# Attention in smaller portions, layers in groups of two units

## The chip, the cores and the metric

The kernel runs on one core of one Trainium2 chip. A core has TensorE (matmuls), VectorE, ScalarE and GpSimd (elementwise work), SyncE (here it issues DMAs), and 16 DMA engines. The metric is the device time of one execution in microseconds (us); less is better.

## The reference

There are three stages. The first is a linear attention with a complex decay: for each of 4 x 8 heads, over 768 steps t,

```python
S_re = ar * S_re - ai * S_im + outer(k[t], v[t])
S_im = ar * S_im + ai * S_re_old
y[t] = q[t] @ S_re
```

where ar and ai are a_re and a_im scaled to a magnitude of at most 0.999, and a head has 48 dimensions. The result is laid out as x, 3072 tokens by 384. The second and third stages are two layers, each with weights of 384 x 2048 and 2048 x 384: `x = softplus(x @ w_in) @ w_out`, then `elu(x @ w_in2) @ w_out2`. All is computed to float32 accuracy, and the weights are given in 64-bit floats.

## The kernel before, in words

Each matmul of the layers is done as three (`Net.PASS`): both operands are split into a high and a low part (`split`, line 398), and high x high, high x low and low x high are added up.

**Units, items, slots.** The 3072 tokens are cut into 12 units of 256. Attention works through the units in order (`decays`, line 849, with `norm`, `prep` and `qk`: products of decays, mostly on VectorE; `chunks`, line 802: its matmuls). One layer for one unit is an item, 24 in all, in the order that `PHASES` (line 421) gives: a triple (m, a, b) is layer m for units a to b - 1. The 2048 hidden columns of an item are done in 8 slots, so the main loop (line 935) runs over 192 slots and two more. Slot n issues the first matmuls of slot n (`s1`, 18 of them), the elementwise work of slot n - 1 (`elem`: ScalarE, then VectorE at line 563 or 566, ScalarE, GpSimd at line 571) and the second matmuls of slot n - 2 (`a_s2`, 18, or `b_s2`, 12). At an item's end `a_out` copies the result and stores it to x2d in DRAM from ScalarE's queue (line 588), or `b_out` stores the final output from SP's. `x_load` (line 921) loads an item's input during the item before, at its third slot, and it is split at its sixth.

**Pace.** `adv(ns)` (line 896) hands out attention: it raises a counter of what is due, and runs attention's generators until the time that `Paced` has added up for attention's VectorE instructions has reached it. `Paced` counts (elements + 70) / 0.96 ns for each (line 27). Each slot calls `adv` twice with `STEP`: twice 2000 ns up to slot 43, twice 1600 from slot 44 (`LATE`) on. Ahead of slot 0 it is called with 6000 (`W0`) until unit 0 is through, with one granule of weights decoded after each call, up to 12. The order in which the program issues instructions is their priority; each engine's own order is made from it by a scheduler when the kernel is built.

**Weights.** A layer's weights are 32 granules of 128 x 384. `w_load` loads one as raw 64-bit floats into one of three raw tiles, wr0 to wr2, `decode` (lines 437 to 444, ScalarE and VectorE) makes a float32 of it, and `w_end` splits it (ScalarE, and GpSimd at line 400). `w_step` does this for the next granule. Four granules make a weight tile w of 1.5 MB, one for each slot of an item; there are eight buffers, so only one layer's weights are held. The first layer's granules are decoded ahead of the slots that need them (line 941). The second layer's are decoded from slot 10 on, at most `R` a slot (line 972), each tile as its buffer comes free. During the first group of each layer `w_store` writes each tile to DRAM (wd, line 500). Whenever the next group of items has the other layer, `w_again` (line 505) reloads the eight tiles during the last item of the group, one a slot, into the buffer just used, six slots ahead of its first use. The first two groups need none, so 48 tiles are reloaded. While no raw granule is in work, attention's decay norm borrows the raw tiles (`more`, line 154; `Net.free`, `Net.spare`).

Of the kernel before, what the change touches and what calls it, by code (L numbers as in the profile page):

```python
# [397 lines left out]
def split(nc, hi, lo, x, eng=None):  # L398
    nc.scalar.activation(out=hi, in_=x, func=AF.Copy)  # L399
    (eng or nc.vector).tensor_tensor(out=lo, in0=x, in1=hi.bitcast(F32), op=ALU.subtract)  # L400
# [7 lines left out]
CH0 = 7  # L408
DLY = 2
W0 = 6000  # L410
STEP = (2000, 1600)
LATE = 44
G0 = 12
GA = 4
R = 3
KT = 7
QT = 0
NS = 2
XU = 2
LD, SP = 2, 5  # L420
PHASES = ((0, 0, 2), (1, 0, 2), (0, 2, 5), (1, 2, 5), (0, 5, 9), (1, 5, 9), (0, 9, 12), (1, 9, 12))


def decode(nc, f, S, raw, odd=None):
# [323 lines left out]
def all_fine(nc, pp, sp, f):  # L748


    for a, b, lim, op in ((0, 12, 2000.0, ALU.is_le), (12, 28, 1e-16, ALU.is_ge), (28, 92, 0.3, ALU.is_le)):
        nc.vector.tensor_scalar(out=f[:, a:b], in0=f[:, a:b], scalar1=lim, scalar2=1.0, op0=op, op1=ALU.mult)
    g, o = f[:, 94:95], f[:, 95:96]
    nc.vector.tensor_reduce(out=g, in_=f[:, 0:92], axis=mybir.AxisListType.X, op=ALU.min)
    nc.vector.memset(o, 1.0)
    nc.tensor.matmul(out=pp[0:1, 0:1], lhsT=g, rhs=o, start=True, stop=True)
    n = sp.tile([1, 1], I32, name="n_fine")
    nc.vector.tensor_copy(out=n, in_=pp[0:1, 0:1])
    return n


def body(tc, q, k, v, a_re, a_im, w_in1, w_out1, w_in2, w_out2, out):
    nc = tc.nc
    keep = tc.tile_pool(name="keep", bufs=1)
    with keep as keep:
        fine = quick(tc, keep, q, k, v, a_re, a_im, w_in1, w_out1, w_in2, w_out2, out)
        n = nc.values_load(fine[0:1, 0:1], min_val=0, max_val=128)
        with tc.If(n < 128):
            general(tc, q, k, v, a_re, a_im, (w_in1, w_out1, w_in2, w_out2), out)


def quick(tc, keep, q, k, v, a_re, a_im, w_in1, w_out1, w_in2, w_out2, out):
    nc = tc.nc
    with ExitStack() as ctx:
# [4 lines left out]
        def bank(n):  # L779
            i = cnt[n] = cnt.get(n, -1) + 1  # L780
            t = nb[n][i % len(nb[n])]
            return psp.tile([128, 512], F32, name=t, tag=t)
# [3 lines left out]
        net = Net(tc, ctx, flags[:, 28:92], bank, ((w_in1, w_out1), (w_in2, w_out2)))  # L786
# [6 lines left out]
        def xparts():  # L793
            return [xp.tile([128, 3, 256], F32R, name=n, tag=n) for n in ("xh", "xl")]
# [101 lines left out]
        def adv(ns):  # L896

            nonlocal due
            due += ns
            while A.vec.ns < due:  # L900
                if next(st, END) is END:
                    due = A.vec.ns
                    return False
            return True
# [11 lines left out]

        items = [(m, u) for m, a, b in PHASES for u in range(a, b)]
        ends = {sum(b - a for _, a, b in PHASES[:i + 1]) - 1: i for i in range(len(PHASES))}
        starts = {0: 0, **{e + 1: i + 1 for e, i in ends.items()}}

        def x_load(m, u):
            t = net.tp.tile([128, 768], F32, name="xr", tag="x2e").rearrange("p (c t) -> p c t", c=3)
            if m:
                src = net.x2d[:, :, u * 256:(u + 1) * 256]
            else:
                while u not in done:
                    adv(1000)
                src = A.st.pop(("xd", u)).rearrange("(c p) t -> p c t", p=128)
            nc.sync.dma_start(out=t, in_=src)
            return t  # L930

        H, G = {}, {}
        acc, xr, fine, more = None, None, None, True
        N = 8 * len(items)
        for n in range(N + 2):
            i, p = n // 8, n % 8
            if n < N:
                m, u = items[i]
                while (m, u) not in X:
                    adv(1000)  # L940
                while net.g < min(32, 4 * n + GA):
                    net.w_step()
                if net.g == 32:
                    net.w_end()
                H[n] = net.s1(m, p, X[m, u])
            el = None
            if 0 <= n - 1 < N:
                el = net.elem(items[(n - 1) // 8][0], H.pop(n - 1))
                next(el)
            more = adv(STEP[n >= LATE])  # L950
            if n >= 2:
                i2, p2 = (n - 2) // 8, (n - 2) % 8
                m2, u2 = items[i2]
                if p2 == 0:
                    acc = [bank("acc0"), bank("acc1")]
                (net.b_s2 if m2 else net.a_s2)(p2, G.pop(n - 2), acc)
                if p2 == 7:
                    if m2:
                        net.b_out(u2, acc, out)
                    else:  # L960
                        net.a_out(u2, acc)
                if starts.get(i2, 9) < 2:
                    net.w_store(8 * m2 + p2)
                j = ends.get(i2, 0) + 1
                if i2 in ends and 2 <= j < len(PHASES):
                    net.w_again(8 * PHASES[j][0] + p2)
                if 8 <= n - 2 and net.g < 64:
                    if net.g == 32 and not net.raw:
                        net.w_load(32)
                        net.w_load(33)  # L970
                    room = 64 if i2 > 1 else 32 + 4 * p2 + 4
                    for _ in range(min(R, room - net.g)):
                        net.w_step()
                if net.g == 64:
                    net.w_end()
            if el:
                next(el)
            more = adv(STEP[n >= LATE])
            if el:
                G[n - 1] = next(el)  # L980
            if n < N and i + 1 < len(items) and items[i + 1] not in X:
                if p == LD and items[i + 1] >= (0, XU):
                    xr = x_load(*items[i + 1])
                if p == SP and xr is not None:
                    X[items[i + 1]] = x = xparts()
                    split(nc, *x, xr)
                    xr = None
            if fine is None and not more and net.g == 64 and net.f is None:
                fine = all_fine(nc, bank("h"), keep, flags)
# [29 lines left out]
```

## Time and profile before

| | us |
|---|---|
| median of 3 runs (lowest to highest) | 1260.63 (1256.4 to 1266.76) |
| the profiled execution, its own time | 1262.47 |
| its span, from the first to the last instruction | 1260.4 |
| TensorE matmuls busy | 1043.7 (83%) |
| VectorE busy | 766.7 (61%) |
| ScalarE busy | 679.9 (54%) |
| GpSimd busy | 358.2 (28%) |
| DMA moved | 216.89 MB, 172 GB/s |
| mean granted clock of TensorE | 0.934 |

The profile is of one execution. PE is TensorE's matmuls and PEld its weight loads, DVE is VectorE, ACT is ScalarE, POOL is GpSimd, SP is SyncE. A line of a stretch gives its start and end, its length, then for PE, PEld, DVE, ACT and POOL the busy time with the number of instructions, the clock granted to TensorE (1.00 is its upper level of 2.4 GHz, 0.50 the lower of 1.2), the busy share of the DMA engines and GB/s. The ends of the stretches are starts of every eighth of the elementwise instructions that lead a slot's work on ScalarE, so a stretch is eight slots of elementwise work or a multiple. A line of the timeline gives start, duration, engine, line, operation, and in brackets the idle time before it and what ended it.

### The profile page before, as it was taken

The page shows a single profiled execution, that of the slowest core. Times are in us where ns is not written, and L with a number is a line of the kernel's source. Part 1 is how long each engine was busy: PE and PEld are TensorE (multiplying, and loading weights), DVE is VectorE, ACT ScalarE, POOL GpSimd, SP SyncE. Part 2 cuts the span into 40 slices and gives each one's busy share as a digit, 9 for nine tenths or more (in the row PEclk, how much of TensorE's full clock was granted, in tenths as well). Part 3 has the DMA queues.
Part 4 walks back from the last instruction along what each step waited for, and adds up shares of the span by engine and source line. Part 5 has one row for each costly group of instructions (what it writes and reads, how often), then busy time and mean ns, then how long its engine had stood idle before and what let it go on. Part 6 is the DMA issues. An engine that isn't in the chain of part 4 may idle for free.

```text
span 1260.4 us, 20406 instructions
## 1 busy us (share of the span) xinstructions
PE 1043.7 (83%) x7914; PEld 1004.9 (80%) x7914; DVE 766.7 (61%) x1329; ACT 679.9 (54%) x1199; POOL 358.2 (28%) x275
## 2 busy tenths in 40 slices
PE   0007698936777899898799799999999999999997
PEld 0006698825667898798798699899999999999997
DVE  4887998879878799898789789411212222112211
ACT  4545657525567466654464445456644445665443
POOL 2433432203344221222232122223232322322322
PEclk9997799867787999899899799999999999999999
DMA  6677755356986963459855898600740047029000
GB/s 157 206 211 247 232 157 150 83 166 193 298 264 211 348 221 90 139 171 323 271 151 139 208 297 240 194 21 19 290 161 26 26 178 273 26 90 349 26 14 16
DMA packets 115722, 216.89 MB, mean 172 GB/s; under 512 B 50849, under 2 KB 86945, under 8 KB 107425
## 3 DMA queue, kind: packets, MB, share of 16 engines
q1 hardware_dynamic: 102496, 206.85, 51.7%
q10 hardware_dynamic: 13120, 8.65, 2.4%
q8 instruction: 64, 1.05, 0.3%
q14 instruction: 42, 0.34, 0.1%
HBM read 154.14 MB, written 61.34 MB: 171 GB/s over the span
## 4 chain that ended last, share of the span: by engine, by line
PE 48%; DVE 17%; DMA 11%; issue 5%; ACT 4%; POOL 1%; SPq 0%; ACTq 0%; DVEq 0%; POOLq 0%
PE b L536 43%; DVE tmp L28 5%; DMA w<-wd 4%; DVE big L28 3%; PE b L329 2%; DMA wr<-in_moe_w_in_dram 2%; DVE wr L28 2%; DVE W L28 1%; DVE X L28 1%; DMA wr<-in_moe_w_out_dram 1%; DMA kT<-dk 1%; DVE f L443 1%; PE b L353 1%; PE b L390 1%; DMA ai<-in_a_im_dram 1%
## 5 line engine op out<-in xcount | busy, mean ns | idle before, releaser
L536 PE MATMUL b<-xh,w 128*128 128x256 f32 x2304 | 451.2, 293 | 32.3 <-ACT w L399 11.6
L571 POOL TENSOR_TENSOR gl<-t,gh 128x512 fp32r<-128x512 f32 x192 | 267.8, 1395 | 706.6 <-ACT gh L569 690.9
L536 PEld LDWEIGHTS b<-xh,w 128*128 128x128 f32 x2304 | 379.5, 199 | 39.0 <-ACT w L399 13.0
L536 PE MATMUL b<-xl,w 128*128 128x256 f32 x1152 | 334.3, 291 | 0.0
L536 PEld LDWEIGHTS b<-xl,w 128*128 128x128 f32 x1152 | 228.9, 199 | 0.9 <-issue 0.9
L536 PE MATMUL b<-w,gh 128*128 128x384 f32 x768 | 203.1, 348 | 27.3 <-ACT gh L569 19.2
L536 PE MATMUL b<-gh,w 128*128 128x256 f32 x1152 | 219.5, 290 | 3.3 <-ACT gh L569 1.7
L569 ACT ACTIVATE gh<-t 128x512 fp32r<-128x512 f32 x192 | 121.2, 631 | 167.1 <-DVE t L563 74.5
L536 PEld LDWEIGHTS b<-gh,w 128*128 128x128 f32 x1152 | 183.4, 197 | 5.0 <-ACT gh L569 2.1
L566 DVE SCALAR_TENSOR_TENSOR t<-t,b 128x512 f32<-128x512 f32 x96 | 65.7, 685 | 186.7 <-ACT t L560 184.7
L536 PE MATMUL b<-gl,w 128*128 128x256 f32 x576 | 164.1, 290 | 2.8 <-POOL gl L571 2.8
L536 PEld LDWEIGHTS b<-w,gh 128*128 128x128 f32 x768 | 139.8, 197 | 29.9 <-ACT gh L569 21.1
L563 DVE SCALAR_TENSOR_TENSOR t<-b,t 128x512 f32<-128x512 f32 x96 | 65.8, 686 | 147.7 <-PE b L536 119.4
L400 POOL TENSOR_TENSOR w<-f,w 128x384 fp32r<-128x384 f32 x64 | 88.6, 1394 | 186.1 <-ACT w L399 186.1
L536 PE MATMUL b<-w,gl 128*128 128x384 f32 x384 | 130.9, 347 | 3.0 <-POOL gl L571 3.0
L536 PEld LDWEIGHTS b<-gl,w 128*128 128x128 f32 x576 | 111.6, 196 | 4.8 <-POOL gl L571 4.1
L291 PE MATMUL b<-eye,big 128*96 128x128 f32 x112 | 20.3, 329 | 110.0 <-DVE big L28 103.7
L559 ACT ACTIVATE t<-b 128x512 f32<-128x512 f32 x96 | 57.0, 595 | 92.1 <-PE b L536 89.3
L291 PEld LDWEIGHTS b<-eye,big 128*96 128x96 f32 x112 | 14.5, 150 | 113.8 <-issue 103.0
L555 ACT ACTIVATE t<-b 128x512 f32<-128x512 f32 x96 | 57.0, 594 | 60.5 <-PE b L536 50.5
L536 PEld LDWEIGHTS b<-w,gl 128*128 128x128 f32 x384 | 74.0, 195 | 5.3 <-POOL gl L571 4.9
L329 PE MATMUL b<-qT,kT 96*128 96x128 f32 x384 | 58.3, 307 | 9.2 <-ACT kT L293 6.1
(112 smaller groups left out, 1457.6 us busy)
## 6 DMA issues: line engine op xcount, KB each, us to landing
w<-wd SPq DMA_DIRECT2D x48, 1536.0 KB
wd<-w SPq DMA_DIRECT2D x16, 1536.0 KB
wr<-in_moe_w_in_dram SPq DMA_DIRECT2D x32, 384.0 KB
wr<-in_moe_w_out_dram SPq DMA_DIRECT2D x32, 384.0 KB
dq<-big SPq DMA_DIRECT2D x12, 768.0 KB
qT<-dq SPq DMA_DIRECT2D x36, 256.0 KB
kd<-big SPq DMA_DIRECT2D x12, 768.0 KB
KN<-kd SPq DMA_DIRECT2D x20, 384.0 KB
```

Source lines behind the costliest of these rows:

```text
L28: return f(*a, **kw)
L291: nc.tensor.transpose(out=ps[0:96, 128 * i:128 * i + 128], in_=W[:, 96 * (4 * g + i):96 * (4 * g + i) + 96], identity=self.eye)
L329: self.nc.tensor.matmul(out=sc[:, h, :], lhsT=KT[:, 4 * g + h, :], rhs=QT[:, 4 * g + h, :], start=(h == 0), stop=(h == 3), skip_group_chec ...
L353: nc.tensor.matmul(out=o, lhsT=V[:, 48 * h:48 * h + 64], rhs=Pt[h // 4][:, h % 4, :], start=(h < 2), stop=(zs is None and h > 5), skip_gro ...
L400: (eng or nc.vector).tensor_tensor(out=lo, in0=x, in1=hi.bitcast(F32), op=ALU.subtract)
L536: self.nc.tensor.matmul(out=out, lhsT=lhsT, rhs=rhs, skip_group_check=True, **kw)
L555: nc.scalar.activation(out=t, in_=h, func=AF.Abs)
L559: nc.scalar.activation(out=t, in_=h, func=AF.Relu, scale=-1.0)
L563: nc.vector.scalar_tensor_tensor(out=t, in0=h, scalar=0.0, in1=t, op0=ALU.max, op1=ALU.add)
L566: nc.vector.scalar_tensor_tensor(out=t, in0=t, scalar=-1.0, in1=h, op0=ALU.add, op1=ALU.max)
L569: nc.scalar.activation(out=gh, in_=t, func=AF.Copy)
L571: nc.gpsimd.tensor_tensor(out=gl, in0=t, in1=gh.bitcast(F32), op=ALU.subtract)
```

## The change

Three settings change, and one condition. `STEP` becomes three steps: twice 2000 ns a slot up to slot 7, twice 900 up to slot 19, twice 1250 after. `PHASES` becomes twelve groups of two items, six of each layer in turn; as every group but the first two is preceded by a reload of eight tiles, 80 tiles are reloaded. `R` falls from 3 to 2. Ahead of the first matmuls of a slot in the second layer, granules are now decoded until that slot's tile is there (36 + 4p of them).

```diff
-STEP = (2000, 1600)
-LATE = 44
+
+STEP = ((8, 2000), (20, 900), (999, 1250))
...
-R = 3
+R = 2
...
-PHASES = ((0, 0, 2), (1, 0, 2), (0, 2, 5), (1, 2, 5), (0, 5, 9), (1, 5, 9), (0, 9, 12), (1, 9, 12))
+PHASES = tuple((m, u, u + 2) for u in range(0, 12, 2) for m in range(2))
...
-                while net.g < min(32, 4 * n + GA):
+                while net.g < min(32, 4 * n + GA) or m and net.g < 36 + 4 * p and net.g < 64:
                     net.w_step()
...
-            more = adv(STEP[n >= LATE])
+            more = adv(next(ns for to, ns in STEP if n < to))
...
-            more = adv(STEP[n >= LATE])
+            more = adv(next(ns for to, ns in STEP if n < to))
```

## Rows read from the trace of the kernel before

**Rows 1.** The page: sums, and busy tenths in 40 slices.
```profile
PE 1043.7 (83%) x7914; PEld 1004.9 (80%) x7914; DVE 766.7 (61%) x1329; ACT 679.9 (54%) x1199; POOL 358.2 (28%) x275
...
PE   0007698936777899898799799999999999999997
...
DVE  4887998879878799898789789411212222112211
```

**Rows 2.** The page, the chain that ended last, by line.
```profile
PE b L536 43%; DVE tmp L28 5%; DMA w<-wd 4%; DVE big L28 3%; PE b L329 2%; DMA wr<-in_moe_w_in_dram 2%; DVE wr L28 2%; DVE W L28 1%; DVE X L28 1%; DMA wr<-in_moe_w_out_dram 1%; DMA kT<-dk 1%; DVE f L443 1%; PE b L353 1%; PE b L390 1%; DMA ai<-in_a_im_dram 1%
```

**Rows 3.** Busy times by stretch: start and end, length, engines (instructions), clock, DMA.
```profile
132.10:197.70 65.60, 54.92 (x451) 51.38 (x450) 63.09 (x107) 40.36 (x76) 22.80 (x16) 0.90 0.56 167
...
397.00:841.80 444.80, 404.41 (x3211) 388.86 (x3212) 362.15 (x618) 238.72 (x393) 107.40 (x73) 0.95 0.68 204
197.70:397.00 199.30, 139.44 (x929) 125.98 (x928) 158.09 (x272) 113.46 (x232) 57.67 (x47) 0.78 0.65 202
...
397.00:480.70 83.70, 75.13 (x537) 72.80 (x538) 74.39 (x131) 53.67 (x90) 22.61 (x16) 0.96 0.72 250
480.70:545.20 64.50, 57.73 (x504) 54.45 (x503) 60.04 (x115) 37.36 (x62) 14.60 (x9) 0.95 0.38 106
545.20:640.40 95.20, 84.61 (x667) 81.63 (x666) 78.33 (x114) 48.81 (x82) 24.68 (x16) 0.95 0.86 267
640.40:688.80 48.40, 46.76 (x371) 44.97 (x370) 47.50 (x82) 24.68 (x41) 10.51 (x7) 1.00 0.47 119
688.80:787.50 98.70, 87.33 (x649) 85.12 (x648) 83.34 (x158) 49.16 (x81) 23.95 (x16) 0.91 0.88 252
787.50:841.80 54.30, 52.85 (x496) 49.89 (x495) 18.55 (x23) 25.04 (x44) 11.06 (x9) 1.00 0.45 123
841.80:876.40 34.60, 34.60 (x291) 34.60 (x290) 6.95 (x9) 21.41 (x36) 10.42 (x9) 1.00 0.07 24
876.40:945.00 68.60, 68.60 (x541) 68.60 (x541) 13.33 (x18) 37.76 (x63) 21.16 (x17) 1.00 0.55 208
945.00:978.80 33.80, 33.80 (x242) 33.80 (x241) 7.46 (x10) 16.11 (x26) 10.35 (x8) 1.00 0.07 24
...
1218.00:1260.40 42.40, 35.75 (x246) 35.43 (x244) 6.61 (x10) 15.87 (x26) 10.33 (x8) 0.96 0.06 21
```

**Rows 4.** Source line 353, attention's output matmuls: durations in ns, first and last start.
```profile
L353 PE MATMUL b<-P,V x384: 270/273/477, 101.0 to 826.7; 128*64 128x128 f32 x192
```

**Rows 5.** Instruction groups of all the span: the first layer's elementwise sum, the decode.
```profile
L563 DVE SCALAR_TENSOR_TENSOR t<-b,t 128x512 f32<-128x512 f32 x96 | 65.8, 686 | 147.7 <-PE b L536 119.4 <-ACT t L557 28.3
...
L443 DVE SCALAR_TENSOR_TENSOR f<-wr,f 128x384 int32<-128x384 int32 x64 | 43.9, 691 | 0.7
L444 DVE SCALAR_TENSOR_TENSOR f<-wr,f 128x384 int32<-128x384 int32 x64 | 39.7, 625 | 0.6
L441 DVE TENSOR_SCALAR f<-wr 128x384 int32<-128x384 int32 x64 | 38.1, 600 | 35.4 <-DMA wr<-in_moe_w_in_dram 14.8 <-POOL w L400 11.1 <-DMA wr<-in_moe_w_out_dram 9.5
```

**Rows 6.** Timeline of ScalarE from 602; below, busy times of two stretches there.
```profile
602.38 0.52 ACTq L588 DMA_DIRECT2D x2d<-x2e  x1
602.95 0.84 ACT L141 ACTIVATE wr<-wr 128x768 f32<-128x768 f32 x1 [11.63 <-DMA w<-wd]
...
591.00:601.40 10.40, 6.30 (x30) 5.81 (x30) 4.38 (x8) 0.32 (x2) 0.00 (x0) 0.84 1.08 256
601.40:608.20 6.80, 3.35 (x11) 3.09 (x12) 2.54 (x4) 4.38 (x8) 1.28 (x1) 0.50 1.02 311
```

**Rows 7.** Timelines of VectorE (decode, two products) and of SP (one load).
```profile
243.78 0.36 DVE L441 TENSOR_SCALAR f<-wr 128x384 int32<-128x384 int32 x1 [2.58 <-DMA wr<-in_moe_w_in_dram]
...
268.60 0.96 DVE L28 TENSOR_TENSOR W<-ar,wr 128x768 f32<-128x768 f32 x1
...
283.66 0.63 DVE L441 TENSOR_SCALAR f<-wr 128x384 int32<-128x384 int32 x2 [8.17 <-DMA wr<-in_moe_w_out_dram]
...
270.45 0.36 SPq L484 DMA_DIRECT2D wr<-in_moe_w_out_dram  x1
```

## The prediction

> **What bounds the kernel now.** I read the slices of the page first, to see where TensorE is not full: its digit is 9 all along only from the 24th slice on, and two slices later the digit of VectorE falls from 9 to 4 and then 1 [rows 1]. So there are two regimes, with attention and without it. Then I read the busy times by stage, cut at the first elementwise instruction of ScalarE of every eighth slot, and last the chain, to learn which waits end late: 43% of the span hangs on the two layers' matmuls and 4% on the reload of weights, w<-wd [rows 2].
>
> Without attention, eight slots (an item) take 34.6 us in the first layer and 33.8 (33.9 over several) in the second, TensorE is busy all of that time at a granted clock of 1.00, and this is so with a reload (68.6 us for two items) as without one [rows 3]. That is the floor. With attention, 397.0 to 841.8, nine items take 444.8 us: VectorE is busy 362 us of them, the DMA engines 68%. Worst are slots 8 to 23, where the second layer's weights are decoded: 199.3 us for 16 slots, with VectorE busy 158 us, TensorE 139 us at a mean clock of 0.78 [rows 3].
>
> What does a matmul of attention cost? The stage from 787.5 has 496 TensorE instructions where a plain one has 288 (36 a slot), and 18.3 us more busy time, so 0.089 us each [rows 3]. The page counts 7914 matmuls [rows 1], of which 12 x 288 + 12 x 240 = 6336 are the layers', so attention has about 1578, some 131 for each of its 12 units.
>
> **How the work is handed out.** The counter of line 27 gives 32.1 us for a unit up to the seventh and 33.8 after, 393.6 in all; 72.9 of it are handed out when slot 0 starts. Before: 44 slots at 4.0 us take 176, the other 144.7 go at 3.2 a slot, which ends at slot 89; the trace's last attention matmul, at 826.7, lies in slots 88 to 95, so the count holds [rows 3, 4]. After: 8 slots at 4.0 (32.0), 12 at 1.8 (21.6), the other 267.1 at 2.5, which ends at slot 127. The real time on VectorE is longer. Of its 766.7 us [rows 1], 192 elementwise instructions of the layers take 0.686 each, 131.7, the decode's three instructions 121.7 (1.9 us a granule) [rows 5], splits and output copies about 33; 480 are left, 1.22 times the counter.
>
> **The change stage by stage.**
>
> Start and slots 0 to 7: the same pace, 132.1 + 65.6 us as now [rows 3].
>
> Slots 8 to 23. Handed out are 32.0 instead of 64.1 us of attention, so VectorE loses 32.1 x 1.22 = 39 us and has 158 - 39 = 119 us. The decode keeps its 32 granules, two a slot, and the new loop adds two more ahead of the matmuls in each of slots 21, 22 and 23, since 32 + 2 x 11 = 54 granules are issued by the end of slot 20 and slot 21 needs 56. The first matmuls of these slots wait for a decode just issued; behind them on TensorE stand the second matmuls of two slots back, and ScalarE and GpSimd wait in turn. Lower bound: VectorE's 119 us. Upper bound: those 119, the 41 us in which it idles now, and 5 for the three late slots, 165. I take 145, near the share that VectorE is busy now (119 / 0.79 = 150), a little less because TensorE needs only about 68.5 + 12 us here.
>
> Slots 24 to 127 (13 items, six of the first layer, seven of the second). TensorE: 6 x 34.6 + 7 x 33.9 = 445 us, and nine of the twelve units, 1183 x 0.089 = 105 us: 550. VectorE: 257 x 1.22 + 13 x 7 = 405 us, so it no longer sets the time. What is lost on top? I take each stage of rows 3 with attention, less its items' floor and its matmuls' 0.089 us. The three pairs of items with a reload lose 83.7 - 68.5 - 0.8 = 14.4 us (from 397.0), 95.2 - 68.5 - 12.4 = 14.3 (from 545.2) and 98.7 - 68.5 - 10.8 = 19.4 (from 688.8); the three single items lose 10.7, 2.8 and 1.2. In the first pair VectorE is busy 89%, a limit that thinner attention lifts. The second pair shows the other kind: ScalarE is idle for 11.63 us, until a reload has landed, and only then, at 602.38, issues the store x2d<-x2e that its copies had made ready [rows 6]. From 591.0 to 608.2 TensorE is idle for 7.6 us, and after the gap the granted clock is 0.50 for 6.8 us [rows 6].
>
> The new order of layers has a reload in every second item, 80 instead of 48, and seven of these windows lie in the attention stretch, where there were three; the last of them, slots 122 to 129, only by half, so I count 6.5. What does a window carry? Two plain items with a reload hold 0.55 of the DMA engines, without one 0.07, so eight tiles cost (0.55 - 0.07) x 68.6 = 33 us, 4.1 each; the single item from 480.7 gives (0.38 - 0.07) x 64.5 = 20 us for 28.7 us of the counter, 23 a unit [rows 3]. A window of eight slots at 5.2 us, 42 us, then has 33 + 8 x 2.5 / 32.8 x 23 + 3 = 50 us of transfers, about as overfull as today's (33 + 18 + 3 in some 47 us). So thinner attention doesn't empty it. A tile issued six slots (31 us) ahead still arrives, since only 8 us pile up; late are small transfers behind the reloads. All of them but ScalarE's stores stand in SP's one queue: qT, kT, KN, x's load and the next raw inputs wait behind a reload that waits for its slot's matmuls. I take 9 us a window, what the second pair's one stall cost with its slow clock (7.6 us idle and part of 3.4): 58 us. Bounds: 20 us in all, if an item loses 1.5 us, between the 1.2 and the 2.8 of the two best single items, and 126 at 19.4 a window. Sum 550 + 58 = 608.
>
> By the Trainium skill ("DMA: Bandwidth & Descriptors", section "Issuing engines are not separate DMA queues"), transfers issued by different engines run on the same 16 DMA engines and interleave. That speaks against more reloads, since another queue gives no way around them; but it would also let ScalarE's small store go between the reload's packets. The trace agrees with the first, while the 11.63 us stand before the issue and so aren't interleaving; by the rule alone the windows would cost little, and the sum would be the first rival's.
>
> Slots 128 to 191: eight plain items, 4 x 34.6 + 4 x 33.9 = 274 us, and 8.5 us of tail (the last item takes 42.4) [rows 3]. Three reloads here hide as now. The store of x2d now comes one slot ahead of the load that reads it in every group, as before in the first alone; between that load and its use lie six slots, 26 us, so I cost it at nothing; without that cover it would be a plain slot, 4.3 us, six times. Unit 3 is the tight one: it is done at slot 33 by the counter and its load is issued at slot 34.
>
> Sum: 132.1 + 65.6 + 145 + 608 + 282.5 = 1233.2 us of span. The profiled execution took 1262.47 us for a span of 1260.4, 2.1 more, and is 1.8 above the median of 1260.63; so about 1234 against the median, 2.1% less.
>
> **The rivals.** *Windows that cost nothing.* If thin attention leaves VectorE and ScalarE so much room that small waits don't reach TensorE, the loss is the lower bound, 20 us: 1195. For it speaks that pairs without attention lose nothing; against it, the 50 us of transfers in 42.
>
> *Reloads as the bound (slower).* Every window costs what the worst costs now, 19.4 us: 676 for slots 24 to 127, 1301 in all. The place is SP's queue and ScalarE's store at the end of a window, where attention's loads and the store stand behind eight tiles. It decides from 13.1 us a window on ((1260.4 - 132.1 - 65.6 - 145 - 282.5 - 550) / 6.5): above that the change is a loss. All three of today's pairs are above it, two of them by little (14.4 and 14.3); against it speaks that VectorE, busy 82 to 89% in them, is part of what they lose, and falls to about 70%.
>
> *The pace doesn't shorten the decode.* VectorE decodes a granule at 243.78 and the next ones at 283.66 [rows 7]: the raw tile of the next granule is lent to attention's decay norm, and the load is issued at 270.45, after the two products that read it (from 268.60). Those products lie at about 128 us of the counter, slot 14 before and slot 21 after. If attention must run that far first anyway, the 86 us up to 283.7 stay, and 31 granules at 2.4 us and the rest make 89 more: 175 us, 1263 in all, no change. Against it: VectorE is free to run that attention early while the decode waits, and TensorE has less to do meanwhile.
>
> **How the numbers follow.** Forecast 0.43, free windows 0.20, decode no shorter 0.17, reloads as the bound 0.20. A measurement of this kernel tells about 1% from no change. The forecast's own range is 1212 to 1256 (slots 8 to 23 between 130 and 160, windows between 7 and 11.5 us), of which a quarter lies above 1248. Of the decode case I put 0.02 to faster and 0.04 to slower, since the rest of its sum has the same spread. So faster by over 1%: 0.32 + 0.20 + 0.02 = 0.54; slower by over 1%: 0.20 + 0.04 = 0.24; the rest, 0.22, within 1%. The range reaches down to the free windows and up to a part of the reload case: 1188 to 1288.
>
> **What would show it.** Right: the stage of slots 8 to 23 at 130 to 160 us with VectorE still its busiest engine; the last attention matmul in slots 127 to 130; VectorE's digits at 6 to 8 up to there; no plain item over 35 us; in the attention stretch a TensorE loss that stands beside DMA shares near 1 and ScalarE's stores. Wrong: a stretch of 13 items under 580 or above 650 us, or a decode stage above 170.

## The result, and the profile after

The change makes the kernel faster: median 1222.99 us (1222.02 to 1228.1, 4 runs) against 1259.8 for the kernel before, a ratio of 0.9709 with a 95% interval of 0.9659 to 0.9759. The profiled execution took 1222.02 us for a span of 1220.3, 40.1 less than before. The forecast was 1234. It was near, but two of its stages were wrong, with opposite signs.

The page of the changed kernel: sums, two rows of slices, and the chain by line.

```profile
PE 1029.5 (84%) x7914; PEld 994.2 (81%) x7914; DVE 769.8 (63%) x1329; ACT 678.1 (56%) x1199; POOL 361.4 (30%) x275
...
PE   0007699937776999999999899999999999999997
...
DVE  4898998888877899595599999881222112221121
...
PE b L536 30%; DMA xr<-xd 1%; PE b L329 1%; DMA V<-in_v_dram 1%; DVE big L28 1%; PE b L353 1%; PE b L390 0%; PE b L356 0%; DVE t L563 0%; DVE W L28 0%; DVE tmp L28 0%; ACT big L233 0%; ACT t L555 0%; ACT t L556 0%; DVE xl L400 0%
```

TensorE's digits are 9 from the 14th slice to the last but one, with one 8 among them; in [rows 1] this is so from the 24th on, with one 7 among them, in the 26th. The dip of slices 9 to 13 stays. The chain can't be set beside [rows 2]: it can be followed back only to 768.5 us, so it tells nothing of the slots before. What the profile has of waits for a reload (w<-wd) in the whole span is below, sum in us, times, longest: two lines of the kernel before, then the only one of the changed kernel, though 80 tiles are reloaded there instead of 48.

```profile
ACT wr L141 <- DMA w<-wd: 11.6, 1, 11.6
PE b L536 <- DMA w<-wd: 2.7, 2, 2.0
```

```profile
ACT gh L569 <- DMA w<-wd: 3.8, 1, 3.8
```

VectorE's digit falls to 1 at 824 us (the 28th slice of 30.5 us), and at 819 before (the 27th of 31.5).

Busy times by stretch of the changed kernel, columns as in [rows 3]: the four stages (slots 0 to 7, 8 to 23, 24 to 127, the rest), then the pairs of items from slot 24 on.

```profile
129.40:194.40 65.00, 52.96 (x443) 49.52 (x442) 62.50 (x107) 39.97 (x75) 22.95 (x16) 0.92 0.57 168
194.40:388.30 193.90, 138.05 (x930) 125.07 (x928) 158.01 (x272) 113.58 (x234) 59.83 (x47) 0.77 0.67 207
388.30:938.60 550.30, 530.68 (x4232) 517.13 (x4233) 393.03 (x656) 307.52 (x506) 151.95 (x105) 0.98 0.76 254
938.60:1220.30 281.70, 275.33 (x2116) 275.01 (x2114) 55.21 (x76) 149.44 (x244) 82.68 (x64) 1.00 0.46 171
...
388.30:467.50 79.20, 73.60 (x517) 71.95 (x518) 71.45 (x120) 48.97 (x82) 25.85 (x17) 0.94 0.75 263
467.50:545.70 78.20, 76.23 (x617) 75.12 (x616) 62.29 (x119) 52.01 (x87) 24.22 (x17) 1.00 0.68 239
545.70:634.10 88.40, 83.53 (x667) 80.49 (x667) 61.06 (x107) 48.96 (x82) 23.59 (x17) 1.00 0.75 240
634.10:733.40 99.30, 94.95 (x782) 92.92 (x781) 94.82 (x153) 56.27 (x92) 25.23 (x17) 0.97 0.87 277
733.40:809.90 76.50, 73.79 (x575) 71.47 (x574) 70.33 (x118) 42.00 (x70) 20.84 (x15) 1.00 0.74 257
809.90:890.40 80.50, 80.37 (x682) 78.95 (x681) 22.98 (x29) 40.43 (x69) 21.94 (x17) 1.00 0.74 249
890.40:972.70 82.30, 82.30 (x681) 80.31 (x680) 16.97 (x25) 39.84 (x66) 20.14 (x16) 1.00 0.61 204
```

The same stage, slots 24 to 127, in the kernel before:

```profile
397.00:978.80 581.80, 541.41 (x4278) 525.86 (x4279) 389.88 (x655) 314.00 (x515) 149.33 (x105) 0.96 0.59 183
```

So the gain lies almost whole in slots 24 to 127, 581.8 to 550.3: TensorE idles 550.3 - 530.7 = 19.6 us of them instead of 581.8 - 541.4 = 40.4, and its busy time is 10.7 lower, at a clock of 0.98 instead of 0.96 and with 46 matmuls less (this stage has one item of the first layer less now). The start took 2.7 us less, the stage of the decode 5.4; the rest is as it was.

Where the time came from shows best at the point where attention has left VectorE. Before, at slot 96 (841.8 us), nothing of attention was left [rows 3]. Now, at slot 104 (809.9 us), VectorE has 14 of attention's 893 instructions left: 31.9 us sooner and eight slots further, which is 34 us of plain slots. Against that stand 324 matmuls of attention still to be done (the groups below), at 0.089 us 29 us, which TensorE takes with almost no idle time (80.37 of 80.50 us, 82.30 of 82.30). 31.9 + 34 - 29 = 37, nearly all of the span's gain of 40. These late matmuls are a tail of attention that hardly needs VectorE. TensorE's attention groups from slot 104 to 127 in the changed kernel:

```profile
L353 PE MATMUL b<-P,V 128*64 128x128 f32 x96 | 10.8, 283 | 0.0
L329 PE MATMUL b<-qT,kT 96*128 96x128 f32 x80 | 10.4, 277 | 0.0
L356 PE MATMUL b<-qT,zs 96*48 96x128 f32 x80 | 8.8, 273 | 0.0
L390 PE MATMUL b<-V,KN 128*96 128x48 f32 x68 | 6.7, 248 | 0.0
```

### The profile page after: what moved, and what is told of

Its sections match the earlier page's. It is cut to its first block, busy times and chain, and to the rows that moved or that the text cites. A ratio compares the mean times of both kernels' runs of the same rounds, so it can differ in the third digit from the quotient of the medians.

```text
span 1220.3 us, 20476 instructions
## 1 busy us (share of the span) xinstructions
PE 1029.5 (84%) x7914; PEld 994.2 (81%) x7914; DVE 769.8 (63%) x1329; ACT 678.1 (56%) x1199; POOL 361.4 (30%) x275
## 2 busy tenths in 40 slices
DMA packets 120329, 267.22 MB, mean 219 GB/s; under 512 B 51360, under 2 KB 87456, under 8 KB 107936
## 5 line engine op out<-in xcount | busy, mean ns | idle before, releaser
L536 PE MATMUL b<-xh,w 128*128 128x256 f32 x2304 | 445.9, 291 | 32.9 <-DVE t L563 10.7
L536 PEld LDWEIGHTS b<-xh,w 128*128 128x128 f32 x2304 | 375.5, 198 | 39.7 <-ACT w L399 12.1
L536 PE MATMUL b<-w,gh 128*128 128x384 f32 x768 | 198.4, 342 | 7.7 <-ACT gh L569 6.5
L566 DVE SCALAR_TENSOR_TENSOR t<-t,b 128x512 f32<-128x512 f32 x96 | 65.6, 684 | 179.0 <-ACT t L560 176.8
L536 PEld LDWEIGHTS b<-w,gh 128*128 128x128 f32 x768 | 136.4, 192 | 9.6 <-ACT gh L569 7.3
L291 PEld LDWEIGHTS b<-eye,big 128*96 128x96 f32 x112 | 15.2, 153 | 109.0 <-issue 102.4
```

Of the source, the lines that this page charges most:

```text
L291: nc.tensor.transpose(out=ps[0:96, 128 * i:128 * i + 128], in_=W[:, 96 * (4 * g + i):96 * (4 * g + i) + 96], identity=self.eye)
L536: self.nc.tensor.matmul(out=out, lhsT=lhsT, rhs=rhs, skip_group_check=True, **kw)
L566: nc.vector.scalar_tensor_tensor(out=t, in0=t, scalar=-1.0, in1=h, op0=ALU.add, op1=ALU.max)
```

## The experiments

Twelve kernels, all timed against the kernel before, whose median was between 1256.87 and 1259.66 in these runs. The table gives what was read of each: the median, the ratio with its interval, the lengths of slots 8 to 23, of slots 24 to 127 and of the rest in the profiled execution, TensorE's idle time in slots 24 to 127 (length less busy time), and the sum of ScalarE's waits of over 1 us just ahead of a store (lines 371 and 588, over the whole span, from the end of ScalarE's instruction before it to the issue).

| kernel | us | ratio (95%) | 8-23 | 24-127 | rest | TensorE idle | store waits |
|---|---|---|---|---|---|---|---|
| before | 1259.8 | 1 | 199.3 | 581.8 | 281.6 | 40.4 | 13.4 |
| after | 1222.99 | 0.9709 (0.9659 to 0.9759) | 193.9 | 550.3 | 281.7 | 19.6 | 4.4 |
| e1 pace alone | 1241.66 | 0.9855 (0.9812 to 0.9899) | 195.3 | 566.0 | 281.3 | 32.7 | 10.2 |
| e2 order alone | 1253.69 | 0.9944 (0.9921 to 0.9966) | 195.2 | 579.1 | 282.0 | 40.4 | 7.9 |
| e3 decode alone | 1273.96 | 1.0109 (1.0077 to 1.0141) | 219.3 | 569.8 | 281.4 | 41.7 | 21.3 |
| e4 nothing lent | 1218.22 | 0.9673 (0.9633 to 0.9713) | 159.9 | 570.5 | 281.7 | 25.3 | 4.5 |
| e5 pace and order | 1222.56 | 0.9723 (0.9684 to 0.9763) | 194.8 | 551.9 | 281.8 | 20.7 | 6.0 |
| e6 late pace 1600 | 1236.96 | 0.9839 (0.9798 to 0.9879) | 194.1 | 567.7 | 282.2 | 35.1 | 15.2 |
| e7 late pace 1000 | 1238.9 | 0.986 (0.9819 to 0.9901) | 191.0 | 541.7 | 306.4 | 30.6 | 25.8 |
| e8 nothing lent, R 3 | 1222.62 | 0.9717 (0.9674 to 0.9759) | 165.7 | 577.3 | 281.9 | 29.4 | 2.9 |
| e9 late pace 1100 | 1239.54 | 0.9847 (0.9821 to 0.9873) | 193.3 | 544.2 | 302.3 | 27.3 | 6.3 |
| e10 groups 2, 2, 4, 4 | 1242.45 | 0.987 (0.9833 to 0.9906) | 194.8 | 566.7 | 282.1 | 30.4 | 16.0 |
| e11 a bump in the pace | 1242.72 | 0.9876 (0.985 to 0.9902) | 194.8 | 565.8 | 282.0 | 33.5 | 16.3 |
| e12 nothing lent, 1100 | 1231.35 | 0.9788 (0.9759 to 0.9818) | 159.8 | 565.5 | 302.5 | 35.7 | 19.0 |

**The parts alone.** In the kernel before, the new `STEP` with its two calls of `adv`:

```diff
-STEP = (2000, 1600)
-LATE = 44
+STEP = ((8, 2000), (20, 900), (999, 1250))
```

> The kernel before with the new pace alone. Theory A (the pace only sets who goes first; VectorE does attention ahead in any case, and the layers' instructions now come first in slots 24 to 127): 1230 to 1248 us, slots 8 to 23 again near 195 us, less TensorE loss after them. In the old groups units 2 to 4 are due at slots 26, 34 and 42 and force some of the old pace there, so not all of the gain of the whole change. Rival B (the order of the layers is what helps, by spreading the dates on which units are due): within 6 us of 1260.

1241.66: the pace alone carries about half of the gain, 15.8 us of it in slots 24 to 127, as Theory A has it; slots 8 to 23 are only 4 shorter. In the kernel before, the new `PHASES` alone:

```diff
-PHASES = ((0, 0, 2), (1, 0, 2), (0, 2, 5), (1, 2, 5), (0, 5, 9), (1, 5, 9), (0, 9, 12), (1, 9, 12))
+PHASES = tuple((m, u, u + 2) for u in range(0, 12, 2) for m in range(2))
```

> The kernel before with six groups of two units of each layer alone, at the old pace. Theory A: attention still goes first up to slot 89, five reloads fall into it, and the time is 1255 to 1285 us. Rival B (the order is what helps): 1220 to 1245 us.

1253.69, just under the one range and far from the other. The 32 tiles more that are reloaded cost nothing that shows, even at the old pace: slots 24 to 127 take 579.1 us instead of 581.8, at a DMA share of 0.75 instead of 0.59, and TensorE idles the same 40.4. In the kernel before, the decode's part alone:

```diff
-R = 3
+R = 2
...
-                while net.g < min(32, 4 * n + GA):
+                while net.g < min(32, 4 * n + GA) or m and net.g < 36 + 4 * p and net.g < 64:
```

> The kernel before with two granules a slot and the new condition alone. Theory A (the decode of slots 8 to 23 is held by a lent raw tile and then by its own chain, not by how many granules a slot may issue): 1256 to 1264 us, slots 8 to 23 at 190 to 203. Rival C (fewer granules a slot let attention and the layers through): those slots under 185 us, 1245 or less.

1273.96, which neither expected: alone this part makes the kernel 1.1% slower. Busy times of e3 in slots 8 to 23 and 24 to 127, then those of attention on VectorE alone (source line 28: its busy time and count, the clock, the DMA share, GB/s) in the first of them:

```profile
195.80:415.10 219.30, 146.10 (x977) 130.81 (x977) 187.58 (x345) 124.53 (x247) 63.31 (x46) 0.77 0.66 203
415.10:984.90 569.80, 528.15 (x4236) 513.49 (x4232) 354.00 (x583) 302.24 (x501) 150.07 (x106) 0.98 0.58 179
```

```profile
195.80:415.10 219.30, 130.64 (x229) 0.77 0.66 203
```

The same reading for the kernel before and then for the changed one:

```profile
197.70:397.00 199.30, 90.10 (x158) 0.78 0.65 202
```

```profile
194.40:388.30 193.90, 90.23 (x158) 0.77 0.67 207
```

A thinner decode lets attention go ahead of it: 229 instead of 158 instructions of attention run on VectorE in slots 8 to 23, 40 us more, and the stage is 20 us longer. The stage after it gets 12 of these back. The two other readings are the most telling of the study: before and after, VectorE ran the same 158 instructions of attention in this stage, though the changed kernel handed out half as much.

**Both together.** The changed kernel with the decode's part undone:

```diff
-R = 2
+R = 3
...
-                while net.g < min(32, 4 * n + GA) or m and net.g < 36 + 4 * p and net.g < 64:
+                while net.g < min(32, 4 * n + GA):
```

> The changed kernel with three granules a slot and without the new condition: pace and order of layers alone. Theory A (with a thin pace VectorE's attention is a filler, so it doesn't matter how many granules a slot may issue): 1218 to 1230 us, slots 8 to 23 at 190 to 198. Rival C (two granules a slot are what the thin pace needs): 1235 us or more.

1222.56, the changed kernel's time, so beside the new pace the decode's part neither costs nor gives. Pace and order are the change; together (35 us, against the 1257.39 timed beside them) they bring more than their parts (18 + 6).

**Why slots 8 to 23 don't shorten.** VectorE decodes a granule of the second layer at 239.35 and the next one at 276.41. The changed kernel's timelines of VectorE and of SP:

```profile
239.35 0.39 DVE L441 TENSOR_SCALAR f<-wr 128x384 int32<-128x384 int32 x1
...
262.82 0.96 DVE L28 TENSOR_TENSOR W<-ar,wr 128x768 f32<-128x768 f32 x1
263.69 0.95 DVE L28 TENSOR_TENSOR W<-ai,wr 128x768 f32<-128x768 f32 x1
...
276.41 0.63 DVE L441 TENSOR_SCALAR f<-wr 128x384 int32<-128x384 int32 x2 [1.87 <-DMA wr<-in_moe_w_out_dram]
```

```profile
264.67 0.35 SPq L484 DMA_DIRECT2D wr<-in_moe_w_out_dram  x1
```

It is the pause of [rows 7], 37.1 us instead of 39.9: the raw tile is lent to attention's decay norm, and its load is issued once the products that read it are through. So in the changed kernel attention was no longer to borrow the raw tiles before the decode is over:

```diff
-        return 32 <= self.g and not self.raw
+        return 64 <= self.g and not self.raw
```

> The changed kernel, but the raw tiles are lent to attention's decay norm only after all 64 granules are decoded, no longer between the two layers' decodes. Theory D (the pause of 37 us in the decode, from 239 to 276, comes from the lent tile): the pause falls under 15 us, slots 8 to 23 take 160 to 178 instead of 194 us, and the time is 1190 to 1210. Rival E (attention must run that far first anyway, or the raw loads are late by themselves): the pause stays and the time is 1218 to 1230.

1218.22: not the total that Theory D expected, but the rival's (at its lower edge), while the stage shortened as Theory D says. Busy times of e4 in slots 8 to 23 and 24 to 127:

```profile
198.20:358.10 159.90, 118.04 (x786) 106.78 (x785) 144.79 (x255) 104.46 (x222) 61.66 (x46) 0.82 0.70 213
358.10:928.60 570.50, 545.25 (x4376) 529.77 (x4377) 403.65 (x666) 313.79 (x517) 154.38 (x106) 0.98 0.77 253
```

The stage falls from 193.9 to 159.9, so lending was worth 34 us of it. The pause under 15 us did not come, though: the one from 239 to 276 is gone, but another stands earlier. VectorE's timeline in e4:

```profile
172.18 0.34 DVE L441 TENSOR_SCALAR f<-wr 128x384 int32<-128x384 int32 x1
...
216.71 0.36 DVE L441 TENSOR_SCALAR f<-wr 128x384 int32<-128x384 int32 x1 [3.15 <-POOL w L400]
```

Two granules are decoded early, the second at 172.18; the third comes at 216.71, after GpSimd's split of the first, and from there on the decode runs, 60 us sooner than in the changed kernel, but with 4.8 us from granule to granule instead of 3.6. But 144 matmuls of attention fewer (930 - 786) run in the shorter stage. They come later, 4376 against 4232: 144 x 0.089 = 13 of the 20 us by which slots 24 to 127 grow, and TensorE's idle time is 6 more. Slots 0 to 7 grow by 4 too. The profiled span is 10 us shorter, the median 5 us, and the intervals overlap: e4 is not clear of the changed kernel. With R = 3 as well:

```diff
-R = 2
+R = 3
...
-        return 32 <= self.g and not self.raw
+        return 64 <= self.g and not self.raw
```

> The changed kernel without lending raw tiles between the two decodes, and with three granules a slot. Theory D (without the lent tile the decode starts when the first weight buffers come free, and then VectorE's share for it sets its speed): three granules a slot put decode ahead of attention, slots 8 to 23 fall from 160 to 135 to 155 us, and the time is 1195 to 1212. Rival E (the decode is held by loads and buffers of its own, 4.6 us a granule in the run without lending): within 4 us of 1218.

1222.62, and the stage takes 165.7 us, so both ranges are missed, the rival's by little. Three granules allowed a slot do not make the decode faster: from its third granule to its last it runs from 215.7 to 356.7 us, in e4 from 216.7 to 357.2.

**How far the pace decides.** The changed kernel with another last step of the pace, first 1600, then 1000, then 1100:

```diff
-STEP = ((8, 2000), (20, 900), (999, 1250))
+STEP = ((8, 2000), (20, 900), (999, 1600))
```

> The changed kernel with twice 1600 ns instead of twice 1250 from slot 20 on, which is the old late pace. Theory A (attention that is handed out faster than VectorE does it goes ahead of the layers and holds them): handed out by slot 103 instead of 127, slots 24 to 127 lose more, 1228 to 1245 us. Rival F (the reloads or the order set these slots, not the pace): within 4 us of 1223.

```diff
-STEP = ((8, 2000), (20, 900), (999, 1250))
+STEP = ((8, 2000), (20, 900), (999, 1000))
```

> The changed kernel with twice 1000 ns from slot 20 on. Theory A: attention is a filler already, so thinner handing out gains little or nothing, until units are due: 1210 to 1226 us. Rival G (units come too late, since they are forced out when their item's load is due): 1230 us or more.

```diff
-STEP = ((8, 2000), (20, 900), (999, 1250))
+STEP = ((8, 2000), (20, 900), (999, 1100))
```

> The changed kernel with twice 1100 ns from slot 20 on; units 5 and 7 are then through three and six slots ahead of their loads, where twice 1000 ns left none and one. Theory H (the 1239 us at twice 1000 come from units that are only just in time, and thinner is better until then): 1208 to 1222 us. Rival I (1250 is thin enough, and thinner gives nothing): 1221 to 1228.

1236.96, 1238.9 and 1239.54. For 1600 the range of Theory A came out, but not its reason: attention was not handed out faster than VectorE does it. By the counter some 216 and 293 us of it were due at slots 48 and 72, and VectorE had run 231 and 320. For 1000 the rival's range came out. Too thin a pace has a plain price: units come late, attention's last matmul lies in slot 151 (1000) or 141 (1100) instead of 128, and the rest takes 306.4 or 302.3 us instead of 281.7. Slots 24 to 127 are shorter in return, but not by as much. With 1000, slots 96 to 103 take 69.5 us at a clock of 0.88, in e7:

```profile
744.60:814.10 69.50, 54.13 (x425) 51.07 (x423) 45.08 (x81) 30.18 (x51) 12.70 (x9) 0.88 0.74 210
```

Its waits of TensorE there (sum in us, times, longest):

```profile
PE b L536 <- ACT gh L569: 7.3, 2, 6.7
PE b L536 <- DMA w<-wd: 5.5, 1, 5.5
```

None of them is a wait for a unit of x. ScalarE, whose gh TensorE waits for, stands for 21.08 us there, ahead of two stores of attention's results:

```profile
768.15 5.96 ACTq L371 DMA_DIRECT2D xd<-ye  x2
774.22 0.60 ACT L555 ACTIVATE t<-b 128x512 f32<-128x512 f32 x1 [21.08 <-DMA dk<-big]
```

For 1100 both ranges failed: it is as slow as 1000. The pace of 1100 was also tried with nothing lent:

```diff
-STEP = ((8, 2000), (20, 900), (999, 1250))
+STEP = ((8, 2000), (20, 900), (999, 1100))
...
-        return 32 <= self.g and not self.raw
+        return 64 <= self.g and not self.raw
```

> The changed kernel without lending between the two decodes and with twice 1100 ns from slot 20 on. If the shorter decode stage and the thinner pace add up: 1200 to 1214 us. If the attention that is not done while the decode waits has to be done later at the layers' cost: 1215 to 1225.

1231.35, outside both ranges, with as long a rest as e9 (302.5 us) and 19.0 us of store waits.

**Fewer reloads, and a bump.** The changed kernel with groups of two, two, four and four units (48 reloads, as before), and with a thicker pace in slots 40 to 47:

```diff
-PHASES = tuple((m, u, u + 2) for u in range(0, 12, 2) for m in range(2))
+PHASES = tuple((m, u, v) for u, v in ((0, 2), (2, 4), (4, 8), (8, 12)) for m in range(2))
```

> The changed kernel with groups of two units twice and of four units twice, so that 48 tiles are reloaded instead of 80; units 0 to 6 and 8 to 11 are handed out as before, unit 7 two slots earlier. Theory J (with a thin pace a reload window costs nothing to speak of): 1217 to 1230 us. Rival K (the windows cost what the forecast took, 9 us each, two fewer of them in slots 24 to 127): 1200 to 1212 us.

```diff
-STEP = ((8, 2000), (20, 900), (999, 1250))
+STEP = ((8, 2000), (20, 900), (40, 1250), (48, 1850), (999, 1250))
```

> The changed kernel, but with twice 1850 ns in slots 40 to 47, which brings units 5 to 11 to the slots at which the old groups with the new pace had them (55, 68, 80, 94, 107, 119, 123). Theory L (the new groups help the new pace only because no unit is forced out early): 1232 to 1246 us, as the pace alone had 1242. Rival M (it is the mixing of the two layers itself): within 5 us of 1223.

1242.45, outside both ranges, and 1242.72. Fewer reloads are not faster: in e10 TensorE idles 30.4 us of slots 24 to 127 at a DMA share of 0.63, against 19.6 at 0.76 in the changed kernel. So it isn't the number of reloads that costs. The bump came out as its theory had it, but e9 and e10, with nothing of the kind, lie at the same time, so this is weak evidence. What e11 does show is the stall of [rows 6] once more, in another place. ScalarE's timeline in e11:

```profile
700.92 0.36 ACT L587 ACTIVATE x2e<-b 128x256 f32<-128x256 f32 x1
...
713.12 0.52 ACTq L588 DMA_DIRECT2D x2d<-x2e  x1
713.75 0.60 ACT L559 ACTIVATE t<-b 128x512 f32<-128x512 f32 x1 [12.46 <-DMA qT<-dq]
```

And e11's busy times around it:

```profile
699.00:717.00 18.00, 9.17 (x61) 8.76 (x61) 2.56 (x5) 4.62 (x9) 2.45 (x3) 0.90 0.89 216
```

The source, x2e, is ready at 701.3; the store is issued at 713.1, after a load of qT has landed. ScalarE stands for 12.5 us, TensorE is busy for 9 of 18 us.

What such a store waits for can be read from the traces, whose instructions name their semaphores (the counters by which engines and DMAs tell each other that something is done). Every DMA of these kernels is given one of eight completion semaphores, which is raised when it has landed; they are used about in turn, 48 or 49 times each for the 386 DMAs of the kernel before. All 14 kernels together have 38 store waits of over 1 us, and in all 38 ScalarE waits for the very semaphore that its store has been given, until the DMA that had it last has landed: at 602.38 in [rows 6] a reload issued at 573.8, in e11 the load of qT issued at 694.8. So the store waits neither for its data nor for the DMA engines. Which transfer it meets follows from the order in which the program issues its DMAs.

**What stays open.** Pace alone, and every neighbour of the changed kernel with the thin pace of slots 8 to 19 and lending, lie between 1237 and 1243; only a pace of 1250 with six groups lies at 1223 (twice, with and without the decode's part). These last 16 us no single setting explains. They go with TensorE's idle time, and that goes roughly with ScalarE's waits ahead of its stores: the four kernels with at most 6.0 us of such waits idle 19.6 to 29.4 us, those with 10 or more idle 30.4 to 41.7. e9 (6.3 and 27.3) fits, e2 (7.9 and 40.4) doesn't. Any setting shifts the order of the DMAs, and so which transfer a store shares its semaphore with. That is a correlation over 14 kernels; no run took these waits away alone, so it isn't shown as the cause.

## Why the prediction was right or wrong

The sum and what was measured, in us of span:

| stage | predicted | measured | difference |
|---|---|---|---|
| start | 132.1 | 129.4 | -2.7 |
| slots 0 to 7 | 65.6 | 65.0 | -0.6 |
| slots 8 to 23 | 145 | 193.9 | +48.9 |
| slots 24 to 127, floor | 550 | 518 | -32 |
| slots 24 to 127, loss | 58 | 32 | -26 |
| rest | 282.5 | 281.7 | -0.8 |

The floor measured is 6 x 34.6 + 7 x 33.9 = 445, and 4232 - (6 x 288 + 7 x 240) = 824 matmuls of attention x 0.089 = 73. The loss is what is left of 550.3. The same working for the kernel before gives 822 matmuls and a loss of 63. (Counted one by one, 850 of attention's matmuls start after this point in both kernels; the stretches cut through slots, which moves 2 us from the loss to the floor.) So the total landed 13 us off only because a stage that was 49 us too short stood against two terms that were 58 too long together. Part of this is one error seen twice, since attention that was taken to wait left one stage and lengthened the next; that the rest fits is luck. Both of the prediction's own signs of being wrong came: 13 items in 550.3 us, under 580, and a decode stage above 170.

**Slots 8 to 23 (wrong).** The step that failed is "Handed out are 32.0 instead of 64.1 us of attention, so VectorE loses 32.1 x 1.22 = 39 us". VectorE lost nothing: 90.23 us and 158 instructions of attention against 90.10 and 158. The calls of `adv` fix only the order of issue, and so the priority; an engine that has nothing more urgent runs attention that was not yet due. By the counter of line 27, some 306 of attention's 893 instructions on VectorE are handed out by slot 24 in the changed kernel and 380 in the one before; 214 + 158 = 372 had run in both. The upper bound of 165 fell with the step. Of the rivals, the one that said the pace doesn't shorten the decode had the mechanism right, as e4 shows: the lent raw tile holds the decode until 276. Its 175 us were too low, because the 31 granules after the pause took 384.3 - 276.4 = 108 us and not 89, with attention still running beside them. Its objection, that VectorE is free to run attention early, is true and was the reason that nothing changed, not a reason for a gain.

**The floor of slots 24 to 127 (wrong by 32 us).** "Nine of the twelve units, 1183" matmuls left at slot 24 come mostly from the same false step: as attention runs ahead of what is handed out, 824 were left (850 counted one by one). A smaller part is the prediction's own count. When 306 of attention's VectorE instructions had run, TensorE had 1106 of its 1578 matmuls left, not 1183; and 257 us of the counter, which the same step used for VectorE, are 65% of its 393.6, or 1030 matmuls.

**The loss there (right in sign, too large).** 9 us a window was the mis-sized term. By the working of the prediction's pairs, the seven pairs with a reload lose 10.7, 1.8, 7.5, 8.2, 3.8, -1.7 and 0.2, 4.4 on average (the first shows 517 matmuls, fewer than the layers' 528, so nothing is taken off there); the three of the kernel before lost 14.4, 14.3 and 19.4. A stretch that cuts through a slot moves such a figure by about 2 us. The argument behind the 9 was that 50 us of transfers don't fit into 42, and that what is late stalls ScalarE and TensorE. The transfers do fit. The seven windows of eight slots in which most of the reloads are issued, from slot 25, 41 and so on to 121, in the changed kernel:

```profile
393.62:433.37 39.75, 38.47 (x258) 37.45 (x258) 33.79 (x75) 21.99 (x38) 12.42 (x8) 0.97 0.81 314
472.02:505.80 33.78, 31.81 (x261) 31.20 (x261) 26.57 (x44) 24.28 (x42) 13.92 (x9) 1.00 0.74 273
551.09:590.47 39.38, 38.23 (x290) 36.98 (x290) 23.89 (x23) 23.06 (x37) 11.67 (x9) 1.00 0.78 233
639.60:688.30 48.70, 44.35 (x360) 43.08 (x359) 45.14 (x81) 28.51 (x49) 13.08 (x9) 0.93 0.92 306
735.48:773.05 37.57, 36.05 (x262) 34.54 (x260) 37.19 (x46) 18.63 (x32) 11.11 (x8) 1.00 0.82 293
814.19:853.62 39.43, 39.30 (x352) 38.30 (x351) 9.87 (x12) 22.48 (x40) 11.60 (x9) 1.00 0.90 312
894.68:942.54 47.86, 47.86 (x404) 45.88 (x403) 10.10 (x15) 19.51 (x33) 9.58 (x9) 1.00 0.75 253
```

Share times length is 25 to 45 us of transfers, not 50, and TensorE idles 10.4 us in all seven together, 1.5 a window. The page's DMA total rose from 216.89 to 267.22 MB in a shorter span. That VectorE's share would fall to "about 70%" was wrong as well. It is 90 to 96% in three of the first five pairs, and those lose 10.7, 8.2 and 3.8. So VectorE is filled with attention there as before; what changed is that the layers' work stands ahead of it. Line 27's counter, added up over the instructions of line 28 as they start, bears this out. At slots 48, 72 and 88 the kernel before had run 249, 331 and 384 us of attention where some 262, 338 and 390 were handed out: it was behind, and what is due stands ahead of the layers' later work. The changed kernel had run 221, 279 and 343 where 197, 257 and 297 were handed out: it was ahead, and what runs ahead fills idle time. e1 and e5 speak for this reading of the pace as a priority; e6, ahead of its pace too (231 of 216, 320 of 293) and yet 14 us slower, shows that it isn't all.

**The free windows (rival, nearest in its stage).** Its loss of 20 us against the measured 32; TensorE's own idle time is 19.6. The rule of the Trainium skill ("DMA: Bandwidth & Descriptors", section "Issuing engines are not separate DMA queues"), that transfers issued by different engines interleave on the same DMA engines, spoke for this rival, and the seven windows above agree, with 1.5 us of idle time each. It doesn't cover the wait before an issue, 11.63 us in [rows 6] and 12.46 in e11. The changed kernel has only 4.4 us of store waits, so what its dearest pairs lose (10.7, 7.5 and 8.2) is not explained by them and stays open.

**Reloads as the bound (rival, wrong).** e2 has all 80 reloads at the old pace and is not slower than the kernel before (1253.69); e10 has 48 at the new pace and is not faster than the changed kernel (1242.45).

**The rest (right).** Slots 128 to 191 and the tail are 281.7 against 282.5, and the last attention matmul was to lie in slots 127 to 130. Source line 353 in the changed kernel, as in [rows 4]:

```profile
L353 PE MATMUL b<-P,V x384: 270/273/476, 98.6 to 936.6; 128*64 128x128 f32 x192
```

936.6 is where slot 128 begins, as the counter had it, though VectorE was through with nearly all of attention by slot 104. The plain items take 33.9 to 34.6 us, under the 35 that the prediction named. The decode's loop ahead of the matmuls cost nothing, as e5 shows, against the 5 us that were in the upper bound.

**Two readings.** "Its digit is 9 all along only from the 24th slice on" passes over the 7 of slice 26. And 18.3 us over 496 - 288 instructions is 0.088 us a matmul of attention, not 0.089; 0.089 goes with the 291 that the plain row shows. Neither moves the sum by 2 us.

## What to carry to other kernels

Work handed out per step of a program is not work done per step: where a scheduler orders instructions by priority alone, count what an engine executed in the stage before taking anything off its busy time. A tile lent to another user delays its owner's next load until that user is through, and shortening the stall pays only as far as the work in its shadow has somewhere else to go. Where an engine that computes also issues DMAs, look at which earlier transfer had the completion semaphore of each of them; an order of issue that keeps such a store away from a slow transfer is the experiment that this study lacks. And the values on either side of a tuned one can both be worse by more than the trend explains (1100 and 1600 cost 17 and 14 us here), so one neighbour's time says little about the mechanism.

## What the runs showed of the hardware

Two things were not expected. A core moved 50 MB more in less time with hardly a wait of TensorE for it: in the last two pairs with attention and a reload, TensorE is busy 80.37 of 80.50 and 82.30 of 82.30 us at DMA shares of 0.74 and 0.61. And a store that is ready can stand 11 to 12 us on the engine that issues it until a transfer issued from another engine has landed (a reload in [rows 6], a load of qT in e11), which holds up all the compute queued behind it on ScalarE. The runs show that this comes from the shared completion semaphore and not from the DMA engines: all 38 such waits of over 1 us are for the store's own semaphore.
